# First batch's q loaded in 1536-byte pieces and put into head order on chip, PSUM tiles of their own for the last output rows, and a new order of work

## The chip, the cores and the metric

One core of one Trainium2 chip runs the whole program. Its engines are TensorE (PE; matmuls and transposes, with PEld its weight loads), VectorE (DVE), ScalarE (ACT), GpSimd (POOL), and SyncE (SP), which here only issues DMA transfers. The metric is the device time of one execution in microseconds (us), lower is better. The kernel before takes 561.53 us, the median of three runs (561.13 to 562.68).

## The reference

Attention whose keys and values are means over 8 tokens, followed by a gated MLP with a mix over tokens. Eight batches, 8 heads of 64, 576 tokens, 512 model columns, 1024 hidden columns.

```python
k_p = k.reshape(B, H, Sp, pool, D).mean(axis=3)          # Sp = 72
v_p = v.reshape(B, H, Sp, pool, D).mean(axis=3)
scores = scale * np.matmul(q, k_p.transpose(0, 1, 3, 2))
attn = softmax(scores)
x = heads_side_by_side(np.matmul(attn, v_p))              # (B, 576, 512)
h = gelu_tanh(x @ w_in)
u, v = h[..., :512], h[..., 512:]
v_n = (v - mean(v)) / sqrt(var(v) + 1e-6) * g_ln
v_s = einsum('ts,bsd->btd', w_sg, v_n) + b_sg[None, :, None]
out = x + (u * v_s) @ w_out
```

q, k, v and w_sg come as float32, w_in and w_out as 64-bit floats, which the kernel turns into float32 pairs by itself.

## The kernel before

The work is cut into steps. A step has a letter, a part number and a batch: C0+0 loads the queries of the first pair of heads of batch 0. A and B load keys and values, E the few rows left over of both (tile `left`); K pools and transposes the keys into `kbd` (for batch 0: an 8-fold sum on PE for most rows, a sum on POOL for the left-over ones, transposes on PE, four scaled copies on ACT); P pools the values; Q puts a pair of heads into `qT`, channels on partitions and tokens along the free axis; S does the scores, their maximum on DVE (`nmax`), twenty-odd small exponentials on ACT and the normalisation on DVE; T and L transpose the weights (`ah`, `al`, `lt`); V multiplies them with the values and splits the result into a high and a low part (`xhl`); H is the second half of the first MLP product with its normalisation (`vg`, `vhh`, `vhl`), U the first half, W the mix over tokens, O the last product, X the last 128 rows of the last batch, Z the stores. Weights are steps in small letters (`v0`: second half of w_in, first piece; `s0`: w_sg; `o0`: w_out; `lv0` is a load): each piece of w_in or w_out is rebuilt by three DVE instructions (L287 to L289), one or two casts on ACT and two or three on POOL or DVE. TensorE products of float32 are done as three products of split parts, which is why everything has a high and a low.

The order in which all steps are issued is written out by hand, in the string `PROLOGUE`, one entry for each part of a step between two `yield`s. Each engine runs its own instructions strictly in that order. All loads go through SP's queue. A second string, `OTHER`, names the places where one engine does an operation in place of another: `copy` (L210) takes DVE in place of ACT, `move` (L216) POOL in place of ACT, `scale` (L222) POOL in place of DVE, `combine` (L236) DVE in place of POOL.

Batch 0 is handled in its own way. `load_q` (L351) reads q in pieces of one head and one token, 64 floats or 256 bytes, tokens on partitions, three transfers for a pair of heads, into four tiles `qnat`. `step_Q` (L516) turns each with five 128-column transposes and one copy. The second large load of w_in waits in SP's queue behind these.

PSUM tiles come from two rings of two: `mtile` (`mps`) and `atile` (`aps`). In the scores of batch 0, the reciprocal of the sum is kept in the same PSUM tile as the scores (L576). Step X turns the last 128 columns of the residual by four transposes, does 24 matmuls into the two halves of one `mps` tile, adds the halves to the residual on DVE (L847) and stores them from two queues.

## Time and profile before

| | before |
|---|---|
| median of three runs | 561.53 us |
| the profiled execution | 560.36 us |
| its span | 558.7 us |
| PE busy | 538.1 us (96%) |
| DVE busy | 435.2 us (78%) |
| ACT busy | 330.6 us (59%) |
| POOL busy | 260.8 us (47%) |
| first matmul | 4.49 us |
| first matmul of step H (batch 0) | 51.84 us |
| first matmul of step W (batch 0) | 94.23 us |
| last matmul starts | 554.67 us |

The span runs from the first to the last instruction in the profile, and 1.7 us of the execution lie around it. Granted clock of PE is full throughout. PE is the engine with the most work, so what it idles is what can be gained without taking work away. The page cuts the span in forty slices, and PE's row is full but for the first three and the last.

### The profile page before, as it was taken

Reading aid. Unit: us, or ns where it says so; the run is one execution under the profiler, and the core shown is the slowest. Engines: PE = TensorE matmul, PEld = TensorE weight load, DVE = VectorE, ACT = ScalarE, POOL = GpSimd, SP = SyncE. Lnnn points to the kernel's source line nnn. Section 1 sums busy time; section 2 is a strip of 40 time slices with the busy share of each in tenths; the row PEclk is TensorE's granted clock in tenths of the full one; section 3 lists DMA queues with packets and bytes.
Section 4 is the critical chain, followed back from the end, with each engine's and each line's share of the span. In section 5 each row is a group of like instructions: output and inputs, shape, how many; then the busy total and the mean of one; then the engine's idle time right before and its main releaser. Section 6 shows DMA issues by size and latency. Waiting matters only on the chain.

```text
span 558.7 us, 10694 instructions
## 1 busy us (share of the span) xinstructions
PE 538.1 (96%) x3677; PEld 508.7 (91%) x3677; DVE 435.2 (78%) x644; ACT 330.6 (59%) x1077; POOL 260.8 (47%) x322
## 2 busy tenths in 40 slices
...
GB/s 246 315 298 164 93 120 76 69 145 122 158 147 90 93 155 146 138 111 134 166 104 158 86 177 162 119 48 151 122 169 99 95 44 83 78 59 2 32 13 106
DMA packets 186470, 68.38 MB, mean 122 GB/s; under 512 B 150576, under 2 KB 170800, under 8 KB 186416
## 3 DMA queue, kind: packets, MB, share of 16 engines
...
## 4 chain that ended last, share of the span: by engine, by line
PE 78%; DVE 9%; ACT 4%; SPq 3%; DMA 3%; issue 1%; POOL 0%; DVEq 0%; ACTq 0%; POOLq 0%
PE mps L139 66%; PE aps L139 12%; SPq L240 3%; ACT e L564 2%; DMA kvraw<-in_k 1%; ACT L207 1%; DVE vg L739 1%; DVE bst L733 1%; DVE al L649 0%; DMA al<-tfar 0%; DVE top L237 0%; DMA lfar<-y 0%; DVE e L223 0%; DVE raw L228 0%; DVE wsl L320 0%
## 5 line engine op out<-in xcount | busy, mean ns | idle before, releaser
L564 ACT ACTIVATE e<-aps,nmax 128x72 f32<-128x72 f32 x280 | 85.0, 354 | 6.3 <-DVE nmax L545 6.2
L139 PE MATMUL mps<-xhl,wih 128*128 128x288 f32 x512 | 88.2, 294 | 0.0
L139 PE MATMUL mps<-wih,xhl 128*128 128x512 f32 x256 | 84.7, 396 | 0.6 <-DVE wsl L320 0.3
L139 PEld LDWEIGHTS mps<-xhl,wih 128*128 128x128 f32 x512 | 75.5, 188 | 1.0
L237 POOL TENSOR_TENSOR glo<-u,ghi 128x576 fp32r<-128x576 f32 x29 | 42.4, 1478 | 69.9 <-ACT ghi L214 35.5
L564 ACT ACTIVATION_READ_ACCUMULATOR e<-aps,nmax 128x1 f32 x280 | 67.4, 242 | 0.0
L237 POOL TENSOR_TENSOR xhl<-x,xhl 128x576 fp32r<-128x576 f32 x30 | 43.8, 1471 | 41.9 <-ACT xhl L692 37.6
L139 PEld LDWEIGHTS mps<-wih,xhl 128*128 128x128 f32 x256 | 48.1, 188 | 11.1 <-ACT u L771 0.7
L139 PE MATMUL mps<-wsh,vhl 128*128 128x288 f32 x256 | 55.1, 296 | 0.3 <-DVE vhl L237 0.3
L139 PE MATMUL mps<-xhl,wil 128*128 128x288 f32 x256 | 54.8, 295 | 0.0
L139 PE MATMUL mps<-wsl,vhh 128*128 128x288 f32 x256 | 54.8, 295 | 0.0
L139 PE MATMUL mps<-wsh,vhh 128*128 128x288 f32 x256 | 54.7, 295 | 0.0
L139 PE MATMUL mps<-ghi,woh 128*128 128x288 f32 (+1 forms) x232 | 51.8, 302 | 0.0
L139 PE MATMUL mps<-ghi,wol 128*128 128x288 f32 (+1 forms) x232 | 50.8, 298 | 0.0
L139 PE MATMUL mps<-glo,woh 128*128 128x288 f32 (+1 forms) x232 | 50.8, 298 | 0.0
L139 PE MATMUL mps<-wil,xhl 128*128 128x512 f32 x128 | 50.1, 391 | 0.0
L785 DVE SCALAR_TENSOR_TENSOR mps<-mps,gcol,bbc 128x576 f32<-128x576 f32 x32 | 26.2, 819 | 27.6 <-PE mps L139 27.6
L237 POOL TENSOR_TENSOR vhl<-vg,vhh 128x512 fp32r<-128x512 f32 x25 | 34.6, 1389 | 23.5 <-DVE vhh L212 18.6
L736 POOL TENSOR_TENSOR rstd<-mv,eps 128x1 f32<-128x1 f32 (+1 forms) x40 | 13.0, 325 | 68.8 <-DVE mv L734 65.5
L646 ACT CAST ah<-al 128x640 fp32r<-128x640 f32 x24 | 17.5, 731 | 41.6 <-DMA al<-tfar 37.9
L139 PEld LDWEIGHTS mps<-wsh,vhl 128*128 128x128 f32 x256 | 41.1, 188 | 0.6 <-DVE vhl L237 0.6
L139 PEld LDWEIGHTS mps<-wsh,vhh 128*128 128x128 f32 x256 | 41.2, 188 | 0.0
(210 smaller groups left out, 1428.8 us busy)
## 6 DMA issues: line engine op xcount, KB each, us to landing
kvraw<-in_k SPq DMA_DIRECT2D x16, 512.0 KB, 4.3
kvraw<-in_v SPq DMA_DIRECT2D x16, 512.0 KB, 4.3
qraw<-in_q SPq DMA_DIRECT2D x112, 72.0 KB, 2.6
out<-y SPq DMA_DIRECT2D x112, 72.0 KB, 2.1
...
```

What stands on the lines that cost most here:

```text
L139: nc.tensor.matmul(o, lhsT, rhs, start=start, stop=stop)
L207: nc.scalar.activation(early, eps[:, 0:1], func)
L237: (nc.vector if key in OTHER else nc.gpsimd).tensor_tensor(o, x, y, op=op)
L240: queue.dma_start(o, i)
L564: nc.scalar.activation(e[:, i, h], slots[i][:, h], AF.Exp, bias=nmax[:, i, h:h + 1], **acc)
L646: nc.scalar.copy(ah, al)
L733: nc.vector.bn_stats(bst, vg)
L736: nc.gpsimd.tensor_tensor(rstd, mv[:, 1:2], eps[:n, 1:2], op=ALU.add)
L739: nc.vector.scalar_tensor_tensor(vg, vg, mv[:, 0:1], rstd.broadcast_to([n, DF2]), op0=ALU.subtract, op1=ALU.mult)
L785: nc.vector.scalar_tensor_tensor(vs, vs, gcol[:, d:d + 1], bbc.rearrange("p (a n) -> p a n", a=2), op0=ALU.mult, op1=ALU.add)
```

## The change

Five things are edited.

1. `load_q` for batch 0 puts six consecutive tokens on one partition: 96 partitions, two heads, 6 x 64 floats or 1536 bytes in one piece; one transfer for a pair of heads. Three pairs go into parts of one tile `first`, which holds the first batch's raw values as well (it lies where `kvraw0` lay), the fourth into `qlast`.
2. `step_Q` for batch 0 first copies the 96 x 768 floats from (head, token, channel) to (token, head, channel) order, on ACT for pairs 0 and 1 and on POOL for 2 and 3, then does six transposes with 96 columns each, and a copy that writes `qT` in order of tokens and reads PSUM with a step of 96 floats.
3. In batch 0, the reciprocal of the softmax sum is always kept in SBUF, so the scores' PSUM tile is free earlier.
4. Step X takes a PSUM tile for each half of the 512 columns, from `mtile` and `atile`, and adds and stores the first half right after its matmuls.
5. A new `PROLOGUE` for batches 0 to 2 and the very end, and a new `OTHER`. From the entries `W0+1 W1+1 V2+2 V1+2` on, 902 entries, the string is the same up to its last line, where one part of X and one of Z3 change places.

```diff
-            t = per.tile([P, NT, 2, D], F32, name="qnat", tag=("e2", "ah", "lt0", "lt1")[g])
-            sv = q[b, 2 * g:2 * g + 2].rearrange("h t d -> t h d")
-            for h in range(2):
-                load(t[:, 0:NT - 1, h], sv[0:S - TAIL, h].rearrange("(i p) d -> p i d", p=P))
-            load(t[:, NT - 1], sv[S - P:S])
+            n = 2 * RUN * D
+            if g == G - 1:
+                t = per.tile([P, n], F32, name="qlast", tag="glo")
+            else:
+                t = first()[:, 4 * POOL * D + n * g:4 * POOL * D + n * (g + 1)]
+            t = t[0:S // RUN].rearrange("p (h f) -> p h f", h=2)
+            load(t, q[b, 2 * g:2 * g + 2].rearrange("h (p i) d -> p h (i d)", i=RUN))
...
-            ps = atile().rearrange("p a n -> p (a n)")
-            for i in range(NT):
-                nc.tensor.transpose(ps[:, i * P:(i + 1) * P], t[:, i].rearrange("p h d -> p (h d)"),
-                                    ident if i < NT - 1 else swap)
-            yield
-            copy(qT, ps[:, 0:S], f"Q{b}{g}")
+            x = x.rearrange("p (i h d) -> p i h d", i=RUN, h=2)
+            src = t.rearrange("p h (i d) -> p i h d", i=RUN)
+            if f"q{g}" in OTHER:
+                nc.vector.tensor_copy(x, src)
+            else:
+                move(x, src, f"r{g}")
+            yield
+            ps = atile()
+            for i in range(RUN):
+                a, j = divmod(i, RUN // 2)
+                nc.tensor.transpose(ps[:, a, j * n:(j + 1) * n], x[:, i].rearrange("p h d -> p (h d)"), ident[0:n, 0:n])
+            yield
+            copy(qT.rearrange("p (q a j) -> p q a j", a=2, j=RUN // 2),
+                 ps[:, :, 0:HALF].rearrange("p a (j q) -> p q a j", q=n), f"Q{b}{g}")
...
-        if key in OTHER:
+        if key in OTHER or b in FIRST:
             rec = ssum
...
-        ps = mtile()[0:n]
-        part = [slice(DM // 2 * k, DM // 2 * (k + 1)) for k in range(2)]
+        y = per.tile([n, DM], F32, name="yrow", tag="qraw0")
+        w = DM // 2
         for k in range(2):
+            ps = (mtile, atile)[k]()[0:n, 0, 0:w]
+            cols = slice(w * k, w * (k + 1))
             for c in range(KC):
-                for j, (w, z) in enumerate([(woh, ghi), (wol, ghi), (woh, glo)]):
-                    mm(ps[:, k, 0:DM // 2], z[:, c, LAST:S], w[:, c, part[k]], c == 0 and j == 0,
-                       c == KC - 1 and j == 2)
+                for j, (r, z) in enumerate([(woh, ghi), (wol, ghi), (woh, glo)]):
+                    mm(ps, z[:, c, LAST:S], r[:, c, cols], c == 0 and j == 0, c == KC - 1 and j == 2)
             yield
-        y = per.tile([n, DM], F32, name="yrow", tag="qraw0")
-        for k in range(2):
-            nc.vector.tensor_tensor(y[:, part[k]], ps[:, k, 0:DM // 2], x[:, part[k]], op=ALU.add)
+            nc.vector.tensor_tensor(y[:, cols], ps, x[:, cols], op=ALU.add)
             yield
-            load(out[b, LAST:S, part[k]], y[:, part[k]], (nc.sync, nc.scalar)[k])
+            load(out[b, LAST:S, cols], y[:, cols], (nc.sync, nc.scalar)[k])
             yield
```

The first lines of the order string, before and after, and the two sets:

```diff
-A0+0 K0+0 A1+0 E0+0 K0+0 lv0 K1+0 v1 v0 K2+0 K1+0 K2+0 K2+0 v1 C0+0 v0 Q0+0 C1+0 Q0+0 S0+0 A1+1 S0+0 C2+0 B1+0 Q1+0
+C0+0 A0+0 K0+0 lv0 Q0+0 A1+0 E0+0 K2+0 v1 v1 v0 Q0+0 K0+0 v1 Q0+0 K1+0 C1+0 K1+0 v0 Q1+0 K2+0 Q1+0 K2+0 S0+0 v0 C2+0
...
-G01 G10 G23 H13 H23 Q01 Q02 Q03 V02 V12 W00 W10 W13 X02 X03 X10 X12 X13 X21 X22 c21 c22 g00 g10 g12 g13 g14 g21 g22
-h01 k31 l1 l2 o0d o2a o2m o3m p30 p31 u0m u1m u2a u2d u3a u3d u3m v0m v1m v2a v2d v2m v3a x11
+G10 G12 G13 G23 H00 H01 H02 H12 H13 H23 K11 P10 Q00 Q01 Q02 Q03 T00 V00 V02 V03 V11 V12 V20 W00 W02 W03 X00 X02 X03
+X12 X13 X23 Z0 c20 c22 g10 g12 g22 h10 k31 l1 n01 n23 o0m o1m o2d o2m o3a p30 p31 r2 r3 u0a u0d u1m u2d u3a u3m v1d
+v2m x12
```

What the order string and the sets do to SP's queue at the start of the program (`kvraw` keys or values, `left` the left-over rows, `raw` a weight, `qnat`, `first` and `qlast` queries) is shown next, before:

```order
L240 DMA kvraw<-in_k 128x2x512 x2
L240 DMA left<-in_k 32x1x512 x2
L240 DMA left<-in_v 32x1x512 x2
L240 DMA raw<-in_moe_w_in 128x2x1024
L240 DMA qnat<-in_q 128x4x64 x2
L240 DMA qnat<-in_q 128x2x64
```

and after:

```order
L243 DMA first<-in_q 96x2x384
L243 DMA kvraw<-in_k 128x2x512
L243 DMA raw<-in_moe_w_in 128x2x1024
L243 DMA kvraw<-in_k 128x2x512
L243 DMA left<-in_k 32x1x512 x2
L243 DMA left<-in_v 32x1x512 x2
L243 DMA first<-in_q 96x2x384 x2
L243 DMA qlast<-in_q 96x2x384
```

The first load of w_in has moved from the seventh to the third place, the second half of the keys and the four left-over loads from ahead of it to behind it, and queries take four transfers in place of twelve.

DVE's first work after the program's setup, from the second half of the first weight piece on (`top` and `raw` are parts of a weight piece, `nmax` the maximum of the scores, `ssum` the sum of the exponentials), before:

```order
L287 TENSOR_SCALAR mps<-mps 128x512
L288 SCALAR_TENSOR_TENSOR top<-raw,mps 128x512
L289 SCALAR_TENSOR_TENSOR raw<-top 128x512
L545 TENSOR_REDUCE nmax<-mps 128x10
L212 COPY qT<-aps 128x576
L228 SCALAR_TENSOR_TENSOR raw<-raw 128x512
L212 COPY qT<-aps 128x576
L545 TENSOR_REDUCE nmax<-mps 128x10
L571 TENSOR_TENSOR ssum<-ssum,eps 128x10
L577 RECIPROCAL mps<-ssum 128x5x2
L223 TENSOR_TENSOR e<-e,mps 128x720
```

and after, from the same place:

```order
L290 TENSOR_SCALAR mps<-mps 128x512
L291 SCALAR_TENSOR_TENSOR top<-raw,mps 128x512
L292 SCALAR_TENSOR_TENSOR raw<-top 128x512
L215 COPY qT<-aps 128x576
L566 TENSOR_REDUCE nmax<-mps 128x10 x2
L215 COPY qT<-aps 128x576 x2
L592 TENSOR_TENSOR ssum<-ssum,eps 128x10
L598 RECIPROCAL ssum<-ssum 128x10
L226 TENSOR_TENSOR e<-e,ssum 128x720
```

All four copies into `qT` are DVE's now (one stands between the two halves of the piece, ahead of these rows), two maxima come one after the other, and the low part of the weight piece (L228) has gone to POOL.

DVE just ahead of the first step W of batch 0 (`vg` the normalised half, `al` the low part of the transposed weights of batch 1, `vht` the last rows), before:

```order
L635 TENSOR_TENSOR al<-aps,ah 128x576
L739 SCALAR_TENSOR_TENSOR vg<-vg,mv,rstd 128x512 x2
L212 COPY x_1077<-aps 128x576
L635 TENSOR_TENSOR al<-aps,ah 128x576
L528 STREAM_TRANSPOSE qT<-qraw 128x576
L739 SCALAR_TENSOR_TENSOR vg<-vg,mv,rstd 64x512
L635 TENSOR_TENSOR al<-aps,ah 128x576
L753 TENSOR_TENSOR vht<-vg,vht 64x512
```

and after:

```order
L760 SCALAR_TENSOR_TENSOR vg<-vg,mv,rstd 128x512
L215 CAST xhl<-aps 128x576
L656 TENSOR_TENSOR al<-aps,ah 128x576
L754 BN_STATS bst<-vg 64x6
L755 BN_AGGR mv<-bst 64x2
L760 SCALAR_TENSOR_TENSOR vg<-vg,mv,rstd 128x512
L656 TENSOR_TENSOR al<-aps,ah 128x576
L549 STREAM_TRANSPOSE qT<-qraw 128x576
L760 SCALAR_TENSOR_TENSOR vg<-vg,mv,rstd 64x512
L240 TENSOR_TENSOR vhl<-vg,vhh 128x512
```

The two `vg` of whole tiles no longer stand together, a cast into `xhl` has come in between, and DVE forms the low part `vhl` (three of the four of this batch), which POOL did before.

More of the change, by code (lines that the diff above doesn't have):

```diff
@@ L79 @@
[L79 to L80 removed]
+C0+0 A0+0 K0+0 lv0 Q0+0 A1+0 E0+0 K2+0 v1 v1 v0 Q0+0 K0+0 v1 Q0+0 K1+0 C1+0 K1+0 v0 Q1+0 K2+0 Q1+0 K2+0 S0+0 v0 C2+0
+Q2+0 Q1+0 S0+0 C3+0 S1+0 S0+0 Q2+0 Q3+0 S1+0 Q2+0 lo0 o1 S1+0 Q3+0 A1+1 K1+1 S2+0 Q3+0 v0 A0+1 o0 S3+0 S0+0 T0+0 v1
+B1+0 K1+1 K0+1 S2+0 o1 S0+0 S1+0 B0+0 S2+0 S3+0 S3+0 lv1 E0+1 ls0 T0+0 o0 S2+0 K0+1 P0+0 S1+0 v3 S3+0 v3 S2+0 P1+0
@@ new lines @@
+O0+0 S3+2 H1+1 Z2+0 S2+2 H3+1 O0+0 O0+0 H3+1 V2+1 O3+0 O3+0 H2+1 S2+2 H3+1 O3+0 A0+3 S2+2 H2+1 O1+0 C1+3 Z2+0 S3+2
+L0+2 A1+3 T0+2 L0+2 V1+1 H1+1 P2+2 K0+3 H1+1 O1+0 P2+2 H0+1 L0+2 Q0+3 H3+1 H0+1 O1+0 H1+1 U2+1 T0+2 K1+3 L0+2 B0+3
+U2+1 Z0+0 V0+2 L0+2 E0+3 Z0+0 T3+2 K2+3 T1+2 H0+1 H2+1 H4+1 U1+1 T2+2 H4+1 H4+1 T1+2 H0+1 U0+1 Z3+0 H0+1 T1+2 U1+1
+H4+1 H2+1 Z3+0 V1+2 T2+2 H4+1 U0+1 H4+1 U3+1 H4+1 H0+1 H2+1 Z1+0 T2+2 Z1+0 Q1+3 V0+2 H2+1 H4+1 U3+1 T2+2 W1+1 V2+2
+C2+3 K2+3 V1+2 T3+2 T3+2 W0+1 W1+1 V2+2 V1+2 W2+1 K2+3 P0+3 T3+2 V3+2 B1+3 K2+3 V3+2 V2+2 C3+3 W0+1 W2+1 S0+3 V3+2
@@ new lines @@
+Q2+3 S0+3 S1+3 P1+3 W3+1 W1+1 V0+2 W0+1 S0+3 A0+4 S1+3 W3+1 W2+1 C0+4 Q3+3 V2+2 S1+3 S0+3 H2+2 W0+1 H2+2 P2+3 W2+1
+W1+1 U2+2 H2+2 V3+2 S3+3 S1+3 V0+2 S0+3 W3+1 O0+1 W3+1 S3+3 U2+2 S2+3 T0+3 S3+3 P2+3 O0+1 T1+3 S2+3 O1+1 O1+1 V1+2
+P2+3 O0+1 S1+3 S3+3 T0+3 O2+1 S2+3 S3+3 O2+1 O1+1 H1+2 Z1+1 T0+3 P2+3 H2+2 Z1+1 O2+1 O3+1 S2+3 O3+1 H1+2 S2+3 L0+3
+Z2+1 Z2+1 H2+2 H0+2 H1+2 O3+1 L0+3 H2+2 H0+2 K0+4 C1+4 H4+2 A1+4 L0+3 Q0+4 H4+2 T0+3 H0+2 U3+2 H4+2 L0+3 U3+2 T3+3
+V0+3 H3+2 H1+2 H1+2 T1+3 H4+2 H1+2 H3+2 E0+4 U1+2 T1+3 L0+3 U1+2 H4+2 U0+2 T2+3 H0+2 H4+2 H4+2 B0+4 Z0+1 Q1+4 T1+3
@@ L81 @@
+H1+7 O3+6 H2+7 H1+7 H3+7 H0+7 V3+7 H1+7 O3+6 H0+7 V2+7 H4+7 H2+7 H4+7 O3+6 H1+7 H4+7 H4+7 H1+7 Z3+6 U2+7 H0+7 H0+7
+Z1+6 H0+7 U0+7 U2+7 U3+7 U0+7 U1+7 H4+7 H4+7 U3+7 H4+7 U1+7 H4+7 W0+7 W1+7 Z0+6 W0+7 Z0+6 W1+7 W1+7 W2+7 W1+7 W0+7
+W3+7 Z3+6 W0+7 W2+7 W3+7 W2+7 W3+7 W2+7 W3+7 Z2+6 Z2+6 O0+7 O1+7 X0+7 O0+7 O1+7 X0+7 O0+7 Z0+7 O2+7 O2+7 Z0+7 O1+7
+Z1+7 O3+7 O3+7 Z1+7 O2+7 Z2+7 X0+7 Z2+7 O3+7 Z3+7 Z3+7 X0+7 X0+7 X0+7 X0+7 X0+7
 """.split()
@@ L112, in tile_pooled_attn_gmlp @@
     WHOLE = (0,)
+    FIRST = (0,)
     TURNED = (0, 1)
@@ L115, in tile_pooled_attn_gmlp @@
     BAND = 160
+    RUN = 6
     LAST = S - P
@@ L330, in keys, with first @@
         return src.rearrange("(g h) (j r) d -> g (h j) (r d)", h=2, r=POOL)
+    def first():
+        if "first" not in st:
+            st["first"] = per.tile([P, 4 * POOL * D + 3 * 2 * RUN * D], F32, name="first", tag="xhl")
+        return st["first"]
     def load_kv(b, which, gp):
@@ L334, in load_kv @@
         if b == 0 and which == 1:
-            if "kvraw0" not in st:
-                st["kvraw0"] = per.tile([P, 2, 2, POOL * D], F32, name="kvraw0", tag="xhl")
-            t = st["kvraw0"][:, gp]
+            t = first()[:, 0:4 * POOL * D].rearrange("p (a g f) -> p a g f", a=2, g=2)[:, gp]
         else:
```

100 lines of the change are left out of this document (44 added, 56 removed).

## The prediction

> **What bounds the kernel now.** I read first the busy times of the page, then four stretches of the program.
>
> ```profile
> span 558.7 us, 10694 instructions
> PE 538.1 (96%) x3677; PEld 508.7 (91%) x3677; DVE 435.2 (78%) x644; ACT 330.6 (59%) x1077; POOL 260.8 (47%) x322
> ...
> 0.00:11.20 11.20, 6.28 (x34) 6.04 (x34) 0.18 (x1) 2.19 (x4) 6.64 (x25) 1.00 0.83 257
> 11.20:51.80 40.60, 33.94 (x234) 29.08 (x234) 38.28 (x58) 36.38 (x132) 19.33 (x20) 1.00 0.92 266
> 51.80:95.40 43.60, 40.63 (x268) 37.07 (x269) 41.25 (x66) 38.43 (x127) 30.36 (x36) 1.00 0.39 101
> 95.40:300.00 204.60, 204.60 (x1432) 196.81 (x1431) 175.31 (x254) 124.53 (x408) 97.59 (x118) 1.00 0.56 131
> ```
>
> The columns of a stretch are its length, then busy time of PE, PEld, DVE, ACT and POOL, the granted clock, the share of DMA and GB/s. PE idles 558.7 - 538.1 = 20.6 us in all. Of these 4.9 lie in the first stretch (11.20 - 6.28), 6.7 in the second, 3.0 in the third, none from 95.4 to 300. So PE sets the time from 95 us on, and whatever brings its place in the program at 95 us forward is won whole, unless another engine then holds it up. In the second and third stretch DVE is busy for 38.28 of 40.60 and 41.25 of 43.60 us, 94 and 95%: there DVE is the bound, and ACT with 90 and 88% comes next. The list of what PE waited for from 62 to 120 us says the same (total, times, longest):
>
> ```profile
> PE aps L139 <- DVE al L635: 1.2, 1, 1.2
> PE aps L179 <- DVE x L212: 1.0, 1, 1.0
> PE aps L179 <- POOL el L583: 0.6, 1, 0.6
> ```
>
> The three waits on which PE loses 2.8 us end on DVE twice and once on POOL's `el`, which copies DVE's scaled `e`. The question is therefore when DVE can begin, how much it then has to do before the first W, and where it must stand still.
>
> **When DVE begins.** It begins with the first piece of w_in, behind ACT:
>
> ```profile
> 4.41 0.58 SPq L240 DMA_DIRECT2D raw<-in_moe_w_in  x1
> 10.55 1.16 ACT L285 ACTIVATE mps<-raw 128x512 f32<-128x512 f32 x2 [2.01 <-DMA raw<-in_moe_w_in]
> 11.21 0.70 DVE L287 TENSOR_SCALAR mps<-mps 128x512 int32<-128x512 int32 x1 [8.72 <-ACT mps L285]
> ...
> kvraw<-in_k SPq DMA_DIRECT2D x4, 512.0 KB, 4.6
> left<-in_k SPq DMA_DIRECT2D x4, 64.0 KB, 6.7
> ```
>
> Ahead of this load stand two transfers of 512 KB and four of 64 KB, 1280 KB. After the change, 96 x 2 x 1536 bytes (288 KB) of q and 512 KB of keys stand ahead, 800 KB. At the 257 GB/s of the first stretch the 480 KB less are 1.9 us. Bounds: nothing, if the loads behind share the bandwidth evenly; 2.6 us, if the load lands as long after its issue as now (it would be issued at about 1.8 us, after two issues of half a microsecond from 0.80, in place of 4.41). I take **-1.9**, so DVE begins at 9.3 us.
>
> **What DVE has to do.** I compared DVE's rows up to the last `vg` of a whole tile ahead of the first W, before and after. It gains one copy into `qT` and one into `ah`, two copies of 128x128 (`kp`, `vp`), two `vhl` and two low parts of `xhl`. It loses one scaling of `e`, two `wil`, one `wol`, one L228 and one cast into `vhh`.
>
> ```profile
> L212 DVE COPY qT<-aps 128x576 f32<-128x576 f32 x3 | 2.2, 749 | 0.0
> L635 DVE TENSOR_TENSOR al<-aps,ah 128x576 fp32r<-128x576 f32 x4 | 3.0, 749 | 0.4 <-ACT ah L214 0.4
> L237 DVE TENSOR_TENSOR xhl<-x,xhl 128x576 fp32r<-128x576 f32 x2 | 2.5, 1256 | 0.8 <-ACT x L214 0.8
> L237 DVE TENSOR_TENSOR wol<-raw,top 128x512 fp32r<-128x512 f32 x1 | 0.7, 693 | 0.1
> L214 ACT COPY vp<-aps 128x128 f32<-128x128 f32 x2 | 0.5, 263 | 0.0
> L223 DVE TENSOR_TENSOR e<-e,mps 128x720 f32<-128x720 f32 x4 | 3.6, 905 | 0.2
> L237 DVE TENSOR_TENSOR wil<-raw,top 128x512 fp32r<-128x512 f32 x4 | 3.3, 829 | 0.2
> L228 DVE SCALAR_TENSOR_TENSOR raw<-raw 128x512 f32<-128x512 uint32 x8 | 6.3, 786 | 0.0
> L212 DVE CAST vhh<-vg 128x512 fp32r<-128x512 f32 x1 | 0.4, 426 | 0.0
> ```
>
> Gained: 2 x 0.75 + 2 x 0.26 + 2 x 0.69 (`vhl` has the shape of `wol`) + 2 x 0.75 (`xhl` has the shape of `al`) = 4.9 us. Lost: 0.9 + 2 x 0.83 + 0.69 + 0.79 + 0.43 = 4.5 us. That is +0.4; with `xhl` at its own row of 1.26 it is +1.4. I take the middle, **+0.9**.
>
> **Where DVE stands still early.** Its first maximum needs the scores, these need `kbd`, and `kbd` needs the left-over rows, which are now behind w_in.
>
> ```profile
> 7.28 2.07 POOL L395 TENSOR_TENSOR left<-left 64x512 f32<-64x512 f32 x2 [2.06 <-DMA left<-in_v]
> 9.43 0.46 POOL L396 TENSOR_TENSOR lp<-left 64x128 f32<-64x128 f32 x1
> 12.52 0.40 ACT L450 ACTIVATE kbd<-aps 64x288 f32<-64x288 f32 x1 [0.61 <-PE aps L447]
> 13.18 0.38 ACT L453 ACTIVATE kbd<-aps 64x32 f32<-64x32 f32 x2
> 14.28 1.49 PE L139 MATMUL mps<-kbd,qT 128*128 128x144 f32 x10 [1.26 <-ACT qT L214]
> 15.81 0.91 DVE L545 TENSOR_REDUCE nmax<-mps 128x10 f32<-128x720 f32 x1 [0.40 <-PE mps L139]
> ...
> DMA to landing us min/median/max: 3.3/6.3/9.3
> ```
>
> The last line is for all `left` transfers of the first 60 us. The fourth is issued two issues later than now, at about 4.7 us. With the median it lands at 11.0; POOL's 2.6 us (7.28 to 9.89) give 13.6; transposes and `kbd` 1.4 us (some 0.4 us, and 12.52 to 13.56) give 15.0; half of the 1.49 us, since one group of heads is enough (ten rows there are two passes of five), gives 15.8. DVE by then has done two weight halves (three rows from 11.21 to 13.27, 2.06 us each) and two copies of 0.75: from 9.3 to 14.9. The gap is 0.9 us against 0.40 now, **+0.5**. With the shortest landing, 3.3, there is no gap (-0.4); with the longest, 9.3, the gap is 3.9 (+3.5).
>
> **Where DVE stands still later.** PE reaches its first H earlier than it needs DVE's slowest result, since DVE's rows up to that point hardly grow, and then the longest stop of DVE in the third stretch, for H's last rows, goes:
>
> ```profile
> 74.44 0.68 DVE L723 TENSOR_TENSOR vg<-mps,vg 64x512 f32<-64x512 f32 x1 [0.65 <-ACT vg L721]
> ```
>
> **-0.65**, with bounds of 0 and of -2.8, if all of PE's three waits go too. The weights and V steps that PE gets in a new order around them I count at nothing beyond this: it is the same work, and DVE's schedule carries it.
>
> **The end.** DVE adds both halves of the last rows after the last matmul, ahead of the last store:
>
> ```profile
> 555.06 0.76 DVE L847 TENSOR_TENSOR yrow<-mps,xrow 128x256 f32<-128x256 f32 x2 [1.44 <-PE mps L139]
> 546.64 0.62 DVE L810 TENSOR_TENSOR x<-mps,x 128x448 f32<-128x448 f32 x1 [1.91 <-PE mps L139]
> 546.03 0.58 ACT L214 COPY xrow<-aps 128x512 f32<-128x512 f32 x1 [5.49 <-PE aps L832]
> ```
>
> With a tile for each half, the first add runs beside the second half's matmuls, so one of the two 0.42 us rows is left: 0.76 - 0.42, **-0.35**. The copy into `xrow` goes from ACT to DVE, 0.58 us where DVE waits 1.91 us anyhow; without that cover it would cost its 0.58.
>
> **At nothing.** PE has 24 transposes with 96 columns in place of 20 with 128, 2304 columns against 2560, in a stretch in which it idles 6.7 us. The head-order copies have 768 elements a partition:
>
> ```profile
> 13.59 0.64 ACT L214 COPY qT<-aps 128x576 f32<-128x576 f32 x1
> 15.58 1.27 POOL L237 TENSOR_TENSOR top<-top,wih 128x512 f32<-128x512 f32 x1 [5.70 <-DMA qnat<-in_q]
> 8.28 0.27 ACT L214 COPY kp<-aps 128x128 f32<-128x128 f32 x1 [6.21 <-PE aps L139]
> ```
>
> The nearest rows (0.64 us for 576 on ACT, 1.27 for a two-operand 512 on POOL) put them between 0.85 and 1.9 us. ACT's first lies in its 6.2 us of waiting for the first keys, POOL's two in the 5.7 us that POOL idles before 15.6; without cover they would delay the third and fourth scores by up to 1.9. The scaling of `e` on POOL, some 1.9 us (1.27 x 720 / 512), has the same cover, POOL being busy 19.33 of 40.60 us. Twelve q transfers become four, which frees SP and DMA behind w_in; but ACT and DVE take the later weights in their own time, so I count nothing.
>
> **The sum** is -1.9 + 0.9 + 0.5 - 0.65 - 0.35 = -1.5 us. From the profiled execution, 560.36 us (span 558.7 and 1.7 around it), that is 558.9; this execution was 1.2 us below the median of 561.53, on which the same difference gives **560.0**.
>
> **Rivals.** About 0.3% or 1.7 us is what a measurement of this kernel can tell from no change: faster is below 559.85, slower above 563.21.
>
> *DVE is no real bound.* If the stops hide slack that the new order uses, the head start is kept whole and PE's waits for `al`, `x` and `el` go: -1.9 - 2.8 - 0.35 = -5.0, 556.5 us. For it speaks that ACT and DVE each have 5% to 12% idle in these stretches; against it that the order gives DVE more to do, not less.
>
> *The left-over rows come late.* One mechanism at one place: `left` lands 9.3 us after its issue, `kbd` is written at 18 us, the first maximum and the exponentials behind it wait. +3.5 in place of +0.5 gives 563.0; from a landing of 9.6 us on, the kernel is slower by more than 0.3%. It decides when the first exponential starts after 20 us.
>
> *The copies into `qT` are slow,* because they read PSUM with a step of 96 floats. The nearest rows are a sum that reads with a step of 64 floats and the maximum, which reads in order:
>
> ```profile
> L398 DVE TENSOR_REDUCE lp<-left 64x128 f32<-64x1024 f32 x2 | 4.0, 2006 | 0.1
> L545 DVE TENSOR_REDUCE nmax<-mps 128x10 f32<-128x720 f32 x4 | 3.6, 906 | 1.1 <-PE mps L139 1.1
> ```
>
> 1.96 ns an element against 1.26; on a copy of 0.75 us that is +0.42, four times +1.7: 561.7 us. I put only a small chance on it, as the first row's source is SBUF and the second's PSUM. The Trainium skill has a rule of this kind, in "SBUF — State Buffer", section "Door 1: The DMA port swizzle": a line of SBUF holds 16 bytes and one of PSUM two floats, and an access that leaves the line pays. By that rule this rival would be the forecast; the trace has no strided copy out of PSUM that could confirm it.
>
> *It brings no earlier start.* If w_in shares the bandwidth with what stands behind it, the -1.9 goes: 561.9 us.
>
> **Chances.** The forecast 0.34 (of which 0.10 below 559.85), no real bound 0.30, late left-over rows 0.18 (0.12 of it above 563.21), slow copies 0.10 (0.02 above), no earlier start 0.08 (0.02 above). Faster 0.40, same 0.44, slower 0.16. The range goes from the fast rival's 556.5, moved in by 0.1, to 563.3, just beyond the late rows' time.
>
> **What would show it.** Right: w_in's ACT row near 8.7 us and DVE's first weight row near 9.3; the first maximum before 16.5; DVE copies into `qT` of 0.75; the first W at 92.5 to 93.5 us; one add of 0.42 behind the last matmul. Wrong: a first W before 90 (DVE was no bound) or after 95; copies above 1.1; a first exponential after 18.

## The result: 0.9 to 1.2% slower

The changed kernel takes 568.73 us, the median of five runs (566.87 to 569.45), against 561.53 for the kernel before: a ratio of 1.0117, with a 95% interval of 1.0093 to 1.0141. Timed again, beside 17 runs of before on one chip, it was 568.00 against 562.57, 1.0087 (1.0056 to 1.0118). The forecast was 560.0, with a range up to 563.3.

The page of its profiled execution, the lines on the span and the busy times, and the row of the granted clock in forty slices of 14.2 us:

```profile
span 567.0 us, 10687 instructions
PE 541.4 (95%) x3681; PEld 510.7 (90%) x3681; DVE 428.8 (76%) x642; ACT 337.1 (59%) x1090; POOL 260.3 (46%) x319
...
PEclk9999997999999999999999999999999999999999
```

The span grew by 8.3 us; between the medians it is 7.2 and 5.4 us, since the profiled execution of before was a quick one. PE's busy time grew by 3.3 us though its work is nearly the same, and one slice of the clock reads 7: for some time PE worked at a lower clock. The other 5.0 us are idle time of PE. The stretches of the changed kernel, in the columns of the prediction (length; busy PE, PEld, DVE, ACT, POOL; clock; DMA share; GB/s):

```profile
0.00:20.00 20.00, 10.55 (x69) 9.67 (x70) 6.98 (x10) 7.88 (x15) 10.04 (x29) 1.00 0.95 278
20.00:40.00 20.00, 16.63 (x134) 15.34 (x133) 18.26 (x33) 19.18 (x95) 10.63 (x13) 1.00 1.04 295
...
80.00:100.00 20.00, 17.26 (x107) 16.10 (x107) 13.95 (x24) 12.66 (x30) 15.64 (x21) 0.83 0.09 27
100.00:120.00 20.00, 18.08 (x136) 17.61 (x135) 16.20 (x23) 12.16 (x54) 11.06 (x11) 1.00 0.32 75
```

PE's idle time (length less busy) from these rows, and from the same view of before:

| stretch, us | idle before | idle after |
|---|---|---|
| 0 to 20 | 7.7 | 9.5 |
| 20 to 40 | 2.6 | 3.4 |
| 40 to 80 | 1.5 | 1.6 |
| 80 to 100 | 2.8 | 2.7, at a clock of 0.83 |
| 100 to 120 | 0 | 1.9 |
| 120 to 540 | 2.3 | 2.7 |
| 540 to the end | 3.7 | 3.9 |

So there are three places: the opening, 80 to 100 us with its clock, and 100 to 120 us. DVE, the bound by the forecast, was busy for 13.95 us of 80 to 100, where before it was for 19.04.

**The opening.** The timeline of the changed kernel; a row is start, duration, engine, instruction, and in brackets the idle time ahead of it and what ended that:

```profile
9.86 0.70 DVE L290 TENSOR_SCALAR mps<-mps 128x512 int32<-128x512 int32 x1 [7.37 <-ACT mps L288]
12.25 2.02 PE L142 MATMUL aps<-kvraw,ident 128*128 128x128 f32 x16 [1.71 <-DMA kvraw<-in_k]
13.32 2.40 POOL L404 TENSOR_TENSOR left<-left 64x512 f32<-64x512 f32 x2 [8.09 <-DMA left<-in_v]
16.67 0.40 ACT L459 ACTIVATE kbd<-aps 64x288 f32<-64x288 f32 x1 [1.37 <-PE aps L456]
17.16 0.76 DVE L215 COPY qT<-aps 128x576 f32<-128x576 f32 x1 [2.03 <-PE aps L543]
19.10 0.91 DVE L566 TENSOR_REDUCE nmax<-mps 128x10 f32<-128x720 f32 x1 [1.17 <-PE mps L142]
20.04 0.32 ACT L585 ACTIVATE e<-mps,nmax 128x72 f32<-128x72 f32 x1 [1.10 <-DVE nmax L566]
```

DVE's first weight row is 1.35 us earlier than before (11.21). But the second keys are used from 12.25 and the left-over rows from 13.32, both behind w_in, and the first maximum stands at 19.10 in place of 15.81 us. DVE stands still for 2.03 and 1.17 us; the head start is lost, and 3.3 us with it. Single executions differ here: in five other profiles of this opening the first maximum stands between 17.27 and 19.70, and in the profile of tail_only, whose opening is that of before, at 17.07.

**The half clock.** The same view in four equal stretches:

```profile
88.83:92.24 3.41, 1.61 (x13) 1.14 (x11) 2.16 (x4) 1.18 (x2) 3.10 (x5) 1.00 0.52 154
92.24:95.65 3.41, 2.49 (x12) 2.14 (x11) 2.18 (x5) 1.94 (x4) 3.06 (x5) 0.50 0.00 0
95.65:99.07 3.42, 3.42 (x16) 3.40 (x16) 1.53 (x3) 2.50 (x5) 1.93 (x3) 0.50 0.00 0
99.07:102.48 3.41, 3.24 (x24) 3.00 (x23) 2.07 (x4) 1.18 (x2) 3.25 (x5) 1.00 0.00 0
```

PE worked for 1.61 of 3.41 us, and after that had half its clock for twice 3.41 us. A matmul into 288 columns starts 0.13 us after the one before it at 88 us, and 0.24 at 93 (93.15, 93.39, 93.63). PE was busy for 5.91 of these 6.83 us. At full clock that work would take about half, some 3.0 us less, which is nearly all of PE's growth of 3.3. Before, PE was busy for 2.23 us of the stretch that starts at 88.83.

**Two copies out of one PSUM tile.** The rows of DVE, ACT, SP and PE around the two waits at 89 and 108 us; `y<-kp` and `kfar` carry the third batch's keys towards `kbd`:

```profile
89.04 0.75 DVE L215 CAST xhl<-aps 128x576 fp32r<-128x576 f32 x1
89.82 0.64 ACT L217 COPY x<-aps 128x576 f32<-128x576 f32 x1 [3.52 <-DVE xhl L215]
90.51 0.66 PE L182 MATMUL aps<-ident,e 128*128 128x128 f32 x4 [1.23 <-ACT x L217]
99.70 0.65 ACT L217 CAST xhl<-aps 128x576 fp32r<-128x576 f32 x1
100.38 0.76 DVE L215 COPY x<-aps 128x576 f32<-128x576 f32 x1 [2.52 <-ACT xhl L217]
101.05 0.44 DVE L431 STREAM_TRANSPOSE y<-kp 128x256 f32<-128x256 f32 x1
101.71 0.35 SPq L243 DMA_DIRECT2D kfar<-y  x1
110.06 2.72 PE L142 MATMUL aps<-kbd,qT 128*128 128x144 f32 x20 [1.52 <-ACT kbd L450]
```

V's result is read twice, by the cast into `xhl` and the copy into `x`. Where the new set puts one on DVE and the other on ACT (`h10`, `x12`), the second reader starts 0.03 us after the first has ended: one after the other. In the first case ACT stands still for 3.52 us, but most of this is the wait for V's matmuls: where ACT makes the cast too (h10_x12_act), it waits 2.49 us for them, so the split itself costs about 1 us there. In the second case DVE stands 2.52 us, and everything behind it in its queue with it: the keys' transposes, `kfar`, `kbd`, and PE for 1.52 us.

Splitting the readers is not new. The set of before does it too, in two other places (`h01`, `x11`); the rows of before:

```profile
40.34 0.75 DVE L212 CAST xhl<-aps 128x576 fp32r<-128x576 f32 x1
41.12 0.64 ACT L214 COPY x<-aps 128x576 f32<-128x576 f32 x1 [0.48 <-DVE xhl L212]
...
90.66 0.64 ACT L214 CAST xhl<-aps 128x576 fp32r<-128x576 f32 x1 [0.93 <-PE aps L139]
91.33 0.76 DVE L212 COPY x<-aps 128x576 f32<-128x576 f32 x1
```

There too the second reader starts 0.03 us after the first. But it stood still for 0.48 us only, and not at all where DVE was busy until then. What the change made worse is when the second engine gets there.

### The profile page after: what moved, and what is told of

The parts are those of the page before. It is cut to its first block, busy times and chain, and to the rows that moved or that the text cites. A ratio compares the mean times of both kernels' runs of the same rounds, so it can differ in the third digit from the quotient of the medians.

```text
span 567.0 us, 10687 instructions
## 1 busy us (share of the span) xinstructions
PE 541.4 (95%) x3681; PEld 510.7 (90%) x3681; DVE 428.8 (76%) x642; ACT 337.1 (59%) x1090; POOL 260.3 (46%) x319
## 4 chain that ended last, share of the span: by engine, by line
PE 74%; DVE 8%; DMA 8%; ACT 5%; SPq 3%; issue 1%; DVEq 0%; ACTq 0%
PE mps L142 63%; PE aps L142 11%; SPq L243 3%; DMA raw<-in_moe_w_in 2%; ACT e L585 2%; DMA qraw<-in_q 2%; DMA kvraw<-in_k 2%; DMA y<-kfar 1%; ACT L210 1%; DMA tfar<-y 1%; DVE nmax L566 1%; DVE qT L549 1%; DVE raw L231 1%; DVE top L291 0%; DVE raw L292 0%
## 5 line engine op out<-in xcount | busy, mean ns | idle before, releaser
L240 POOL TENSOR_TENSOR xhl<-x,xhl 128x576 fp32r<-128x576 f32 x21 | 31.0, 1479 | 28.8 <-ACT xhl L713 22.8
L142 PE MATMUL aps<-kbd,qT 128*128 128x144 f32 x280 | 38.5, 289 | 5.1 <-DVE e L226 2.2
L142 PEld LDWEIGHTS aps<-kbd,qT 128*128 128x128 f32 x280 | 36.1, 190 | 6.9 <-issue 3.0
```

Of the source, the lines that this page charges most:

```text
L142: nc.tensor.matmul(o, lhsT, rhs, start=start, stop=stop)
L240: (nc.vector if key in OTHER else nc.gpsimd).tensor_tensor(o, x, y, op=op)
```

## The experiments

Each run was timed beside runs of the kernel before on the same chip; the table gives medians, the ratio with its interval, and of the runs how many had a mean clock of 0.999 or more. Of the first five runs of the changed kernel (1.0117, 1.0093 to 1.0141) none was at 0.999.

| run | us | before, us | ratio (95%) | at full clock |
|---|---|---|---|---|
| left_first | 565.57 | 562.73 | 1.0067 (1.0042 to 1.0092) | 5 of 8 |
| fill | 567.79 | 562.73 | 1.0097 (1.0068 to 1.0127) | 1 of 6 |
| pieces_old_order | 566.27 | 562.73 | 1.0075 (1.0052 to 1.0099) | 0 of 6 |
| tail_only | 562.38 | 562.73 | 0.9992 (0.9980 to 1.0004) | 5 of 12 |
| keys_left_first | 570.08 | 562.57 | 1.0124 (1.0090 to 1.0158) | 4 of 6 |
| order_only | 565.79 | 562.57 | 1.0046 (1.0024 to 1.0069) | 3 of 12 |
| other_old | 585.14 | 562.57 | 1.0380 (1.0345 to 1.0415) | 0 of 6 |
| after_again | 568.00 | 562.57 | 1.0087 (1.0056 to 1.0118) | 1 of 6 |
| x12_act | 565.49 | 561.97 | 1.0069 (1.0044 to 1.0095) | 3 of 6 |
| h10_x12_act | 564.55 | 561.97 | 1.0055 (1.0035 to 1.0075) | 0 of 7 |
| left_h10_x12 | 563.24 | 561.97 | 1.0035 (1.0017 to 1.0053) | 9 of 12 |
| natural_left_h10_x12 | 563.20 | 561.97 | 1.0019 (1.0006 to 1.0032) | 10 of 12 |
| s_later_alone | 568.30 | 562.29 | 1.0113 (1.0096 to 1.0131) | 0 of 4 |
| s_later_repairs | 566.25 | 562.29 | 1.0059 (1.0038 to 1.0080) | 2 of 7 |
| s_later_natural | 565.54 | 562.29 | 1.0063 (1.0047 to 1.0079) | 3 of 6 |
| tail_fill | 564.12 | 562.29 | 1.0035 (1.0021 to 1.0049) | 7 of 8 |
| tail_fill2 | 563.19 | 562.04 | 1.0015 (1.0002 to 1.0028) | 12 of 12 |

### The opening

left_first:

```diff
-C0+0 A0+0 K0+0 lv0 Q0+0 A1+0 E0+0 K2+0 ...
+C0+0 A0+0 E0+0 K0+0 lv0 Q0+0 A1+0 K2+0 ...
```

> The changed kernel, with the first batch's four left-over transfers issued right behind the first q and the first keys, ahead of w_in. Theory A (the late left-over rows carry the loss of the opening): the first maximum moves from 19.10 us to 15.5 to 17, the first exponential from 20.04 to 16.5 to 18, and what it gains stays: the first W at 95.5 to 97 in place of 98.72, 565 to 566.5 us in all; if the emptiest stretch of PE fills as well, the granted clock is 1.000 and the time 561 to 563. Theory B (the opening is slack; the loss is made from 85 us on by the half clock and the new order there): the first exponential moves, but the first W and the time stay, 567.5 to 569.5. Cost either way: w_in is issued some 2.9 us later, so DVE's first weight row stands near 12 us in place of 9.86.

Measured: first maximum 17.76 us, first W 95.10, 565.57 us, 1.0067. The time lies in theory A's range, but the first maximum moved by 1.3 us only. The first W moved by 3.6, since there is also no half clock at 90 us in this profile. The interval overlaps that of the second measurement of the changed kernel (1.0087). The left-over rows now start on POOL at 7.87, but PE's row in its timeline shows the next in line, the second keys, which still lie behind w_in:

```profile
12.38 2.02 PE L142 MATMUL aps<-kvraw,ident 128*128 128x128 f32 x16 [1.07 <-DMA kvraw<-in_k]
17.76 0.91 DVE L566 TENSOR_REDUCE nmax<-mps 128x10 f32<-128x720 f32 x1 [0.77 <-PE mps L142]
```

keys_left_first therefore moved both:

```diff
-C0+0 A0+0 K0+0 lv0 Q0+0 A1+0 E0+0 K2+0 ...
+C0+0 A0+0 A1+0 E0+0 K0+0 lv0 Q0+0 K2+0 ...
```

> The changed kernel, with the second keys and the four left-over transfers both ahead of w_in, behind the first q and the first keys. Moving the left-over rows alone brought the first maximum from 19.10 to 17.76 us, and there PE waited for the second keys. Theory A (the opening waits for whichever of keys and left-over rows lands last): the first maximum at 15.5 to 16.5 us, DVE's first weight row at 11.5 to 12.5, and with the clock at 1.000 a time of 563.5 to 565, 1 to 2 us below the 564.7 to 566.1 that the run with the left-over rows first showed at that clock. Theory B (DVE's weight work sets the pace from there on, so a later w_in gives back what earlier scores gain): first maximum earlier, first W and time as in that run, 564.7 to 566.1 at full clock.

Both theories were wrong: the first maximum is later, 21.71 us, and the time 570.08. The rows of ACT and PE in its timeline:

```profile
13.23 1.16 ACT L288 ACTIVATE mps<-raw 128x512 f32<-128x512 f32 x2 [8.33 <-DMA raw<-in_moe_w_in]
14.32 0.26 ACT L217 COPY kp<-aps 128x128 f32<-128x128 f32 x1
...
14.63 3.71 PE L142 MATMUL aps<-kvraw,ident 128*128 128x128 f32 x16 [4.57 <-ACT kp L217]
```

Now w_in lands last, at 13.2 us, and ACT's copy `kp` of the first keys stands behind ACT's weight row in its queue. PE needs the PSUM tile that this copy frees. These 16 matmuls took 3.71 us where the same 16 took 2.02 above, about half the speed, though the clock's row reads 1.00 here. A load that is moved back holds up whatever stands behind its user on that engine.

### The clock

fill puts work into PE's idle time at 90 us:

```diff
             turn(ps, lambda i: ef[:, i])
+            for _ in range({(1, 1): 11, (1, 2): 5}.get((b, g), 0)):
+                mm(ps[:, 2 * NB - 208:2 * NB], wih[:, 0, 0:P], wih[:, 0, 0:208], True, True)
```

> The changed kernel, with 16 matmuls of 208 columns, whose result nobody reads, put behind the transposes of the second batch's attention rows of groups 1 and 2 (11 and 5 of them), into columns of the same PSUM tile that are not used: PE works where it idles at 89.3 to 90.5 and at 91.3 to 91.9 us. Theory C (the clock falls to one half because PE idles for about half of one stretch of 3.4 us): granted clock 1.000, the matmuls of V at 92 to 98 us 0.13 us apart in place of 0.24, the first W at 95.5 to 96.5 in place of 98.72, and the time 3 to 5 us shorter, 563.5 to 566 us. Theory D (the clock falls for another reason, or its fall hides behind DVE and ACT): the clock stays below 1, or the clock is 1 and the time still 567.5 to 569.5.

In its profile there is no half clock at 90 us, the matmuls start 0.13 us apart (92.32, 92.45, 92.58), and the first W stands at 96.56 us in place of 98.72, with nearly the same first maximum (18.95 against 19.10). The median of 567.79 us, though, lies in theory D's range; the 3 to 5 us of theory C did not come.

This one profile does not show theory C either, for four runs without the fill have the same two waits and no half clock there. PE is busy for 1.61 or 1.62 of 3.41 us in left_first (from 87.2 us), keys_left_first (91.7), x12_act (87.0) and s_later_alone, whose stretches are:

```profile
88.80:92.21 3.41, 1.61 (x13) 1.14 (x12) 2.16 (x4) 1.18 (x2) 3.15 (x5) 1.00 0.40 154
92.21:95.62 3.41, 2.28 (x16) 2.05 (x17) 2.85 (x6) 2.31 (x5) 3.02 (x5) 1.00 0.00 0
```

What speaks for theory C is the clock of all runs. 6.83 us at half clock take 0.006 off the mean of a run. Of the 11 runs of the changed kernel 7 have 0.993 or 0.994, of the 6 of fill none (0.996 to 0.999). So a stretch in which PE idles for half of the time makes half clock possible, not certain; what decides, no run here shows.

The price can be read where the program is the same up to the first W: it starts at 98.72 and 98.46 us in the two profiles of the changed kernel, both with half clock at this place, and at 96.69 in s_later_alone, without. That is about 2 us, and fill (96.56) agrees.

after_again is the changed kernel once more:

> The changed kernel again, unaltered, on the chip of these runs, to see its time at more than one clock: 566.5 to 569.5 with a mean clock of 0.994 to 0.997; by theory C (half the clock for one or two stretches of 3.4 us costs 1.5 to 2 us where PE is the bound) runs at a clock of 0.999 or 1.000, if there are any, at 565 to 566.5; by theory D they do not differ.

The one run at 0.999 took 567.15, above theory C's 565 to 566.5; those at 0.993 to 0.994 took 567.9 to 569.3. That is 1 to 2 us in the direction of theory C, on one run.

### Parts alone

pieces_old_order is the kernel before with the new `load_q` and `step_Q`, the old strings, a second entry Q0+0 to Q3+0 ahead of the first, and `r2 r3` in OTHER.

> The kernel before, its order and its choice of engines, with nothing of the change but q's loads in 1536-byte pieces and the copy into head order (groups 0 and 1 on ACT, 2 and 3 on GpSimd), each copy issued where the transposes of that group stood first. If the pieces are harmless and the new order is what loses: within 0.3% of before, 560 to 563. If the pieces or the strided copies lose by themselves: above 563.5, with copies into qT above 1.0 us or scores that wait for the copies.

It lost 3.5 us by medians. The copies into `qT` take 0.64 to 0.76 us, as before, so the strided read costs nothing. What costs is where the copy into head order stands, and the clock:

```profile
14.19 0.83 ACT L223 COPY qnat<-first 96x768 f32<-96x768 f32 x1
...
15.07 1.22 PE L543 MATMUL aps<-ident,qnat 96*128 96x96 f32 x6 [2.00 <-ACT qnat L223]
...
17.02 2.77 PE L142 MATMUL mps<-kbd,qT 128*128 128x144 f32 x10 [0.73 <-ACT qT L217]
19.83 0.91 DVE L566 TENSOR_REDUCE nmax<-mps 128x10 f32<-128x720 f32 x1 [3.82 <-PE mps L142]
```

In the old order the copy lies between `kbd` and the transposes, on the path to the first scores: PE waits 2.00 us for it. At the end of this wait the clock falls to one half, from 14.9 to 21.8 us in this execution. Six transposes take 1.22 us, against 0.66 in the changed kernel, and the ten rows of scores 2.77, against 1.49 in before. So of the 4.0 us by which the first maximum is later than before (19.83 against 15.81), some 1.8 are the clock and the rest is the place of the copy. All six runs were below full clock. The pieces therefore need the order changed, and that change sent the keys behind w_in.

order_only is the changed kernel with `load_q`, `step_Q` and `load_kv` of before.

> The changed kernel, its order and choice of engines, with q loaded as before (twelve transfers of 256-byte rows, no copy into head order). If the loss is made by the order (left-over rows late, half clock, waits around the first W): 565.5 to 569, as slow as the change within 0.5%. If the pieces and their copies carry it: 560.5 to 563.5, first maximum before 17 us.

It lost 3.2 us by medians; at full clock 563.0 to 564.7 on three runs, against 561.2 to 562.8 of before. So the order loses by itself, and so do the pieces in the old order. Whether the pieces add to the loss in the new order stays open: this interval and that of the changed kernel (1.0056 to 1.0118) overlap.

tail_only is the kernel before with the new end alone.

> The kernel before with nothing of the change but its end: PSUM tiles of their own for the two halves of the last rows, the copy into xrow on DVE, the new order of the last entries. One add of 0.42 us behind the last matmul in place of two (0.76 us): 0.35 us shorter, 561.0 to 561.4; by the view that the last store's landing sets the end anyway, no change at all; not slower by more than 0.3 us by either.

0.9992 (0.9980 to 1.0004): at most a gain of about the size forecast, and none that is shown. In the changed kernel's profile the one add is there, and the last store is issued 0.78 us after the start of the last matmul, against 1.18 before (554.67 to 555.85):

```profile
562.86 0.28 PE L142 MATMUL aps<-woh,glo 128*128 128x256 f32 x1
...
563.18 0.42 DVE L867 TENSOR_TENSOR yrow<-aps,xrow 128x256 f32<-128x256 f32 x1 [1.01 <-PE aps L142]
...
563.64 0.36 ACTq L243 DMA_DIRECT2D out<-yrow  x1
```

But from that issue to the end of the span it is 3.4 us, against 2.8 before, in this run and in that of the end alone (557.28 to 560.7): the end took the gain back in both profiles.

other_old is the changed kernel with OTHER of before, and `r2 r3 Z0`.

> The changed kernel with the choice of engines of before (its set OTHER, with the two head-order copies and the last copy as changed): order and loads stay. The opening is the same, so the first maximum stays near 19 us. If the choice of engines makes the waits of 89 to 110 us (DVE's cast of xhl ahead of ACT's copy of x, kbd of the third batch late): PE's idle time from 80 to 120 us falls from 4.7 to under 3 us and the time to 564 to 566.5. If the sequence makes them: same as the change, 567 to 569.5. If the new choice is needed by the new order: above 569.5.

585.14 us: PE waits 5.5 us for one `ah` on ACT and 4.0 for one `vg` on DVE, which it hardly does in either kernel. The set and the order are tuned to each other; taking the whole set back tells nothing of single choices.

### A reader behind another engine's

So single choices were taken back.

```diff
-X12 X13 X23 Z0 c20 c22 g10 g12 g22 h10 k31 ... v2m x12
+X12 X13 X23 Z0 c20 c22 g10 g12 g22 h10 k31 ... v2m
```

> The changed kernel with one choice of engine taken back: the second batch's group 2 copies x from PSUM on ACT (x12 out of OTHER), behind the cast of xhl that ACT makes from the same tile. In the changed kernel DVE stands still for 2.52 us ahead of its copy of x, until that cast ends (100.35), and behind it on DVE stand the two transposes of the third batch's keys, the transfer kfar, and kbd, for which PE waits 1.5 to 2.0 us. Theory E (this stop carries the late kbd): the wait of DVE for ACT's xhl is gone, kfar is issued some 2 us earlier, PE's wait for kbd falls under 0.5 us, and the time is 1 to 2 us shorter than the changed kernel's, 566 to 567. Theory F (kbd is late because GpSimd pools the keys late): PE still waits 1 us or more for kbd and the time stays within 0.5 us.

The median is 565.49 us, half a microsecond below theory E's range, though the interval overlaps that of the changed kernel (1.0056 to 1.0118). In the profile, the fastest of the six runs, the mechanism of theory E is there. DVE's keys wait 0.36 us for POOL, not 2.52 for ACT; `kfar` goes 1.69 us after the first W (94.62) in place of 2.99; PE does not wait for `kbd`, and idles 0 us from 100 to 120. The rows of DVE, SP and ACT (the lines of the program count one less here):

```profile
95.64 0.45 DVE L430 STREAM_TRANSPOSE y<-kp 128x256 f32<-128x256 f32 x1 [0.36 <-POOL kp L404]
...
96.31 0.35 SPq L242 DMA_DIRECT2D kfar<-y  x1
...
101.93 0.42 ACT L445 ACTIVATE kbd<-y 64x256 f32<-64x256 f32 x1 [0.33 <-DMA y<-kfar]
```

From the first W to the last batch's transposes of the residual, which leaves the opening out, it is 452.5 us, against 454.9 in both profiles of the changed kernel and 451.2 before.

h10_x12_act takes back `h10` as well.

> The changed kernel with two choices of engine taken back, x12 as in the run beside it and h10: the second batch's group 0 casts xhl on ACT too, so that ACT's copy of x does not stand behind DVE's cast of the same tile (ACT waits 3.52 us there, to 89.82, and PE 1.2 us for this copy at 89.3 to 90.5). By theory E, kbd as there, PE's wait for x at 89 to 91 us falls from 1.2 to about 0.7 us, PE's emptiest stretch fills a little, and the time is 1.5 to 3 us shorter than the changed kernel's, 565 to 566.5. By theory F 567.5 to 568.5.

564.55 us: as theory E, below its range by 0.4. PE's longest wait for x at 89 us falls from 1.2 to 0.7 us. But PE waits 1.8 us for `kbd` again, though `kfar` is 4.2 us earlier than in the changed kernel: the transfers out of `kfar` landed after 105 us here, some 4 us after their issue (medians 3.9 and 3.7), against 2.9 and 2.8 in the run above. So by how much these choices shorten the time varies with that landing: from the first W on, 453.6.

left_h10_x12 has this repair and that of left_first.

> Both repairs, on the changed kernel: the left-over transfers ahead of w_in, and h10 and x12 on ACT. If the two losses are independent, the 565.6 us of the left-over run less 1.5 to 2.5 us: 563 to 564, within 0.3% of before. If one hides the other: 564.5 to 566.

563.24 us, 1.0035 (1.0017 to 1.0053), clear of the changed kernel's 1.0056 to 1.0118: the two repairs add up. The first maximum is at 16.89, the first W at 93.76, ahead of the profile of before, and 9 of 12 runs are at full clock. This takes back some two thirds of the loss and leaves 1.3 us by the medians, 2.0 by the ratio.

> The same two repairs with q loaded as before (256-byte rows, no copy): what is left is the new order, the new choice of engines and the new end. If the pieces are what keeps the changed kernel slower: 560.5 to 562, at or below before. If the new order itself does: 563 to 565, as left_h10_x12.

563.20 us, 1.0019. With the pieces it was 563.24 and 1.0035, and the intervals overlap: in an order that fits them, the pieces cost 0.9 us or nothing.

### What is left

The one wait of PE that left_h10_x12 has between 100 and 120 us, and before has not, is 1.3 us for `kbd`. The scores that need it were moved behind the first part of W1:

```diff
-... K2+2 Q1+2 K2+2 S1+2 o3 V3+1 S0+2 C2+2 S1+2 S0+2 V0+1 V3+1 W1+0 o3 ...
+... K2+2 Q1+2 K2+2 W1+0 S1+2 o3 V3+1 S0+2 C2+2 S1+2 S0+2 V0+1 V3+1 o3 ...
```

> The changed kernel with one entry of the order moved: the third batch's first two score steps come after the first piece of W1 (12 matmuls of 288 columns a half, about 3 to 4 us of PE work) in place of ahead of it. Theory G (PE waits 1.5 to 2.0 us for kbd because the new order brings it to these scores before the keys can be there): the wait for kbd is gone and the time falls by 1 to 2 us, 566 to 567. Theory H (what PE does not wait there it waits later, since the exponentials and all behind them start later): the wait goes, the time stays within 0.5 us, 567.5 to 568.5.

> The same move on top of the two repairs (left-over rows ahead of w_in, h10 and x12 on ACT; 563.24 us, ratio 1.0035). Theory G: 561.5 to 562.5, ratio 1.000 to 1.002. Theory H: unchanged, 563 to 563.5.

> The same move on the repaired order with q loaded as before (563.20 us, ratio 1.0019; its wait for kbd is 0.5 us). Theory G: 0.5 us less, ratio 0.999 to 1.001. Theory H: unchanged. If this and the run beside it come out alike, the pieces cost nothing once the order fits them; if this one is ahead by over 1 us, they do.

Theory G falls in all three. Alone the move changes nothing; on the repaired kernels it loses 0.24% and 0.44% (1.4 and 2.5 us), which theory H did not foresee either. The last two came out alike, 1.0059 with the pieces and 1.0063 without, which again speaks for pieces that cost nothing there. The wait for `kbd` is gone, and another stands in its place, in the list of PE's waits in s_later_repairs (total, times, longest):

```profile
PE mps L141 <- DVE u L807: 2.6, 1, 2.6
```

and in the stretches of the same kernel:

```profile
109.66:113.07 3.41, 1.40 (x12) 1.19 (x10) 2.84 (x4) 2.25 (x15) 0.81 (x1) 1.00 0.01 2
113.07:116.48 3.41, 2.80 (x12) 2.83 (x13) 3.31 (x7) 3.41 (x25) 0.00 (x0) 0.50 0.00 0
```

W0 needs the PSUM tile that DVE's `u` frees, and `u` stands behind the maxima of these scores on DVE. In this execution, the slowest of its seven, half clock follows this wait too. What makes the remaining 1 to 2 us is open.

Last, the clock in the kernel before. Of its 89 runs beside the experiments 39 had a mean clock of 0.999 or more (median 561.85 us), 38 of 0.996 to 0.998 (562.78). tail_fill is tail_only with 8, 9 and 9 matmuls of 128 columns in PE's waits at 10.4, 13.5 and 21 us; tail_fill2 has 4, 4 and 6.

```diff
             nc.tensor.transpose(ps[0:D, 0, P * g:P * (g + 1)], kp[:, g], ident)
+            if b == 0 and g == 1:
+                for _ in range(8):
+                    mm(ps[:, 1, NB - P:NB], ident, ident, True, True)
...
+            for _ in range((9, 0, 0, 9)[g]):
+                mm(ps[:, 2 * NB - P:2 * NB], ident, ident, True, True)
```

> The kernel before with the new end, and 26 matmuls of 128 columns whose result nobody reads put where PE idles in the opening: 8 at about 10.4, 9 at about 13.5 and 9 at about 21 us. About half of the runs of before show a mean clock of 0.997 or less, and are about 1.2 us slower than its runs at 1.000. Theory C (a stretch of 3.4 us in which PE is idle for half of the time is followed by half the clock): nearly all runs at 0.999 or 1.000, and a median of 560.5 to 561.5, ratio 0.997 to 0.999. Theory D (the clock does not follow PE's idle time): clocks as mixed as those of before, ratio 0.999 to 1.001.

> As the run before it (the kernel before with the new end, and work put into PE's idle time in the opening), with 4, 4 and 6 matmuls in place of 8, 9 and 9: 0.97, 0.97 and 1.46 us by the 0.244 us that one took there, against idle times of 1.19, 1.26 and 1.4 to 1.8 us. Theory C: the clock at 0.999 or 1.000 in nearly all runs, the first scores back at 14.3 us where the keys land as early as in the profile of before, and the time that of the runs of before at full clock less the end's 0.35: 560.5 to 561.5, ratio 0.997 to 0.999. If the clock costs nothing in the opening, where PE waits for others anyhow: ratio 0.999 to 1.001, as the run with the new end alone (0.9992).

The clock follows theory C: 19 of these 20 runs were at 0.999 or more, against 5 of 12 of tail_only, which differs by the fill alone. The time does not: 1.0035 and 1.0015. Part of the price is in the timeline of tail_fill2: the fill lies in the PSUM tile that ACT's copy into `qT` reads next, and the copy waits for it.

```profile
13.47 1.06 PE L139 MATMUL aps<-ident 128*128 128x128 f32 x8
15.26 1.49 PE L139 MATMUL mps<-kbd,qT 128*128 128x144 f32 x10 [0.73 <-ACT qT L214]
```

The profile also shows 1.2 us more of idle PE from 300 to 500 us than the profile of before; why, stays open. No version ran faster than before by more than its interval.

## Why the prediction was wrong

- **What bounds the kernel.** PE as the engine that decides from 95 us on: right, but a place at 95 us is not "won whole" or lost whole. The first W came 4.5 us later (98.72 against 94.23), and from there to the last batch's transposes of the residual another 3.7 us were lost (454.9 against 451.2), 2.3 of them idle time of PE. DVE as the bound of the two stretches ahead: right for before, and carried too far. In the changed kernel no engine is full from 80 to 100 us; a chain of waits is the bound there, so "DVE's schedule carries it" failed.
- **Head start, -1.9.** Measured -1.35 (9.86 against 11.21), within the bounds, and worth nothing: DVE stood still right behind it.
- **What DVE has to do, +0.9.** It did not become more. From its first weight row to its last `vg` of a whole tile DVE was busy for 75.4 us (9.85 to 93.23), before for 75.9 (11.20 to 91.38). What grew is its standing still in that stretch, from 4.2 to 8.0 us.
- **First maximum, +0.5.** This is the first step that failed, a term mis-sized. DVE stood still for 3.20 us ahead of the first maximum in place of the forecast 0.9, so the term is +2.8. Two parts of it were wrong. The median landing of 6.3 us was taken over eight left-over loads of which only four are those of batch 0. These landed in 3.3 to 4.6 us ahead of w_in; behind it they took 8.1 to 9.6, and POOL began at 13.32, not 11.0. And half of the scores' 1.49 us was counted, but the maximum waits for all ten rows: 14.28 + 1.49 = 15.77 and 15.81 in before. The second keys, behind w_in as well, were not in the sum at all; left_first shows that they come next. The rival "left-over rows late" had nearly this size, +3.5, and its sign, a first exponential after 20 us, came true (20.04; 18.21 to 20.64 in the other profiles of this opening). Its time, 563.0, did not, since other losses came on top.
- **Later stops, -0.65, and "at nothing beyond this".** The stop that was named, ahead of `vg` for H's last rows, is gone, but others came: PE's waits from 80 to 120 us grew from 2.8 to 4.6. This is the second step that failed: the premise that the same work in another order and on other engines costs nothing. `x12` and `h10` alone are worth about 0.3% (1.0087 to 1.0055 on one chip; these intervals overlap a little, that of the first measurement, 1.0093 to 1.0141, and that of h10_x12_act do not).
- **The clock.** It was in no term. The profile of before showed 1.00 throughout, and I read that as given, not as something that can change with PE's own waits and from run to run. 1 to 2 us.
- **The end, -0.35.** The step was right (one add, 0.40 us less from last matmul to last store), but no gain in time is shown.
- **Copies into `qT`:** four of 0.75 us, as forecast; the rival of slow copies falls, and for these copies the rule for strided reads that stood beside it. ACT's first head-order copy (0.83 us at 4.07) lay in ACT's waiting time, as said.
- **Marks.** First W at 92.5 to 93.5 forecast, 98.72 measured; "after 95" and "a first exponential after 18" were named as signs of a wrong forecast, and both came.

In sum: the forecast's net change was -1.5 us; the profile's is +8.3. By the runs, the late keys and left-over rows carry 1 to 3 us, the two split readers 1 to 2.5, the half clock 1 to 2, and 1 to 2 us are not explained. That the first two together carry most of the loss is shown by left_h10_x12; how it divides between them and the clock is an estimate, since each repair also changed how often the clock fell.
